# A stored order of tasks, a gate by the tangent, and reciprocals spread by one float32 product

## The chip, the cores and the metric

The kernel runs on one core of one Trainium2 chip. The metric is the device time of one execution, in microseconds; the comparison is between medians of several executions. The core has a matrix engine (TensorE, in the profile PE, with its weight loads as PEld), a vector engine (VectorE, DVE), a scalar engine for activations (ScalarE, ACT), a general engine (GpSimd, POOL) and a queue that issues DMAs (SyncE, SP). Each engine works through its own list of instructions in order and waits on semaphores for the others.

## The reference, cut to what matters

Attention with a positional bias, then a gated block with a short causal convolution (batch 8, 8 heads, sequence 576, head width 64, model width 512):

```python
scores = q @ k.T / 8 + bias            # bias: a two-layer net of log1p distances, 8 heads x 576 x 576
attn = exp(scores - scores.max(-1)); attn /= attn.sum(-1) + 1e-9
x = concat_heads(attn @ v)             # 8 x 576 x 512
gate_pre = sum(conv_w[k] * shift(x, 4 - k) for k in range(5))
gate = 1 / (1 + exp(-gate_pre))
out = (gate * (x @ w_val)) @ w_out
```

## The kernel before, in words

The work falls into tasks. The kernel's text creates them one by one with `add(engines, fn, deps, pri, takes, uses)`: the engines that may run the task, each with a cost, the function that issues its instructions, the tasks it depends on, a priority, and the buffers it takes and uses. Nothing is issued while tasks are created. At the end `Plan.order()` puts all 4162 of them in an order and gives each an engine, and they are issued in that order, so each engine's list is its share of it.

- **Bias**, 36 pieces of 16 rows: `relu` (L374, L376), `bias_mm` (L395), `bias_fin` (L414, L416), `bias_store`.
- **Attention**, 32 `pair(n)`s of two heads of one batch, in 16 runs (`RUNS`, `TRANS`) of two pairs. Per block of 128 query rows: `qkm`/`qkr` (L746, L762) multiply in float32; `logits` (L792, DVE) adds the bias and takes the maximum; `expo` (L804, ACT) exponentiates and sums. Then one of two ways, by `TRANS`. In six runs ("T") `norm` (L857) multiplies by 1/sum, `tp` (L905) transposes on PE and `tev` copies out. In ten runs ("D") the exponentials are split into two float16 parts: `top` (L251 on ACT, L253 on DVE, L255 on POOL) rounds, `rest` and `rest8` (L274, on DVE or POOL) subtract, `swap` transposes by DMA.
- `piece` and `rem_mm` (L974, L1042) multiply with v and `ev` scales the result out. In the D runs 1/sum comes late: `eps` and `recip` (L827, L830) make it, `rh` (L258, L269) and `rl` (L838) split it into two float16 parts, `rb` (L1019; in `rem_mm` L1052) spreads it over partitions by products with a float16 identity, `mu` and `mur` (L1029, L1068) multiply.
- **The gated block** per batch, `mlp`: the convolution (`conv`, `prod`, `acc` at L1114 to L1129, `taps` at L1155 to L1164), `sig` (L1176: the sigmoid, four tiles of 128x576 in one task, in the last batch in four tasks), `split_hi` and `split_lo` (L269, L262, L258, L274), `val` (L1226), `gf` (L1236: the product times a scale per channel `gsc` times the gate), `ghi` and `glo` (L251, L274), `outp` (L1288), `ote` (L1300), `ost`.

`Plan.order()` of the kernel before is a list scheduler: it keeps a clock per engine, counts latencies and costs of its own, and picks by priority. The priorities are tuned numbers (`PAIR_AT`, `PV_AT`, `MLP_AT`, `OFFS`, `LOOK`, `LOAD`). Buffers come from rings (`BUFS`), and the slot a task gets depends on the order too.

```python
def sig(e, ks):
    for k in ks:
        A.activation(out=gates[k].t, in_=gates[k].t, func=AF.Sigmoid)
```

Of the kernel before, what the change touches and what calls it, by code (L numbers as in the profile page):

```python
# [35 lines left out]
SEM, SAME, AHEAD = 0.08, dict(P=0.0, V=0.1, A=0.1, G=0.06, S=0.13), 3.0  # L36
LAT = dict(P=0.16, V=0.08, A=0.09, G=0.03, S=0.0)
SPAN = 3.4
# [3 lines left out]
MLP_AT = (-26, 29, 41, 46, -62, 81, 91, -12)  # L42
PAIR_AT = (-0.25, -8.5, -7.75, -5.5, -7.5, -9, 3.5, -18.5, -6, -0.25, 5.25, 3, -0.5, -3.75, -3.25, -13.25, 7.5, -15, -5.5, -3.25, -8.25, -7.25, 10, 5.5, 13.75, 3, 20.75, 35.75, 32.5, 35.75, 36.25, 48.5)
PV_AT = (-2, -96.5, -90, -28.5, -2.25, -74, -59.75, -8.5, -34.75, -98.25, -19.75, -85, -148.25, -155.25, -53.75, -54.75, 35, -5, -12.75, 64.75, 16.5, -28.75, 24.75, -111, 8.5, 39.75, -12.25, 32.75, 67.5, 21.25, 29.75, -51.25)
TRANS = tuple(x == "T" for x in "TTTTDDDTDDDTDDDD")
# [12 lines left out]
OFFS = dict(qkr=-1.25, ldx=3, swap=-51, qk_ld=-57.75, qkm=5, norm=4, piece=-193, val=-38.5, outp=-128.75, mur=-112.25, bias_store=15.75, conv=-14.25, taps=-12.25, split_hi=-48, rb=30.75, rest=-12, ldv=15.25, w_hi=-57.25, logits=-45.25, relu=-69.5, ost=-236.75, bias_fin=9, ote=-28.5, double_step=-102.25, store=1, ghi=-73.5, sig=-45.5, vtr=-135, recip=-41.25, glo=-8, ev=-66.75, tev=4, evr=-312.75, w_sub=23.75, gf=-165.5, w_ld=-31, mu=-23, w_lo=38.75, bias_mm=-134.5, bias_ld=37.25, expo=-17.25, prod=1.25, vlo=26.25, cw=34, vhi=-0.75, eps=-99.25, vmax=-80.5, acc=1.25, split_lo=11.5, close_bias=-84.5, rem_mm=12.25, top=0, vinv=-26.5, tp=-3.25, vscale=-34, constant=47.25, constant_ev=-204.5, ldm_t=17.25, w_scale=-23.75, bias_ld_t=24.5, qk_ld_t=-52.25, w_max=5.5, cwb=-28, eps_t=-69.5, w_even=-202, ldv_t=23.25, vout=-122.5, vb_store=-79.75, wg_scales=-52, piece_t=-50.75, tp_t=-137, vb_all=62, wg_load=48.25, vmax_t=-102.25, evr_t=62.25, oscale=-56.75, rem_mm_t=45.25, expo_t=-28, vb_max=-170, wg_store=62, w_inv=31.75, recip_t=-178, wg_max=-34.5, qkm_t=4.25, vb_load=-116.25, vmax2_t=-58, norm_t=-8, qkr_t=1.5, ldm=-6, vb_scale=46, wg_inv=58.75, vb_inv=59.75, vmax2=-35.25, logits_t=17.75, ev_t=6.25, tev_t=-169, rl=2, rh=-58.25, rest8=-8.25, wg_mm=32.5, wg_row=52.25, vb_mm=-91)
HOLD = 0.05
STICK = 0  # L60
# [3 lines left out]
RDIV = 2.0**11  # L64
# [11 lines left out]
class Task:  # L76
    def __init__(self, engines, fn, deps, pri, takes):
        self.engines, self.fn, self.deps, self.pri, self.takes = engines, fn, deps, pri, takes
        self.start = self.end = None
        self.late = 0.0  # L80
        self.then = []


class Plan:

# [3 lines left out]
    def add(self, engines, fn, deps=(), pri=0.0, takes=(), uses=(), hold=0.5):  # L94
        name = getattr(fn, "func", fn).__name__
        pri += OFFS.get(name + self.kind, OFFS.get(name, 0.0))
        t = Task(engines, fn, [d for d in deps if d is not None], pri, list(takes))
        t.pri = max([pri] + [d.pri for d in t.deps])
        t.n, t.hold = len(self.tasks), hold
        t.name = name + self.kind  # L100
        t.shares = "GV" if name in SHARED else "G"
        t.mode = MODES.get(name, 0)
        for b in uses:
            b.users.append(t)
        self.tasks.append(t)
        return t

    def order(self):
        free = dict(P=0.0, V=0.0, A=0.0, G=0.0, S=0.0)
        bus = port = 0.0  # L110
        mode, last = 0, None

        pending = {k: [] for k in self.bufs}
        slots = {k: [(0.0, i) for i in range(n)] for k, n in self.bufs.items()}
        for t in sorted(self.tasks, key=lambda t: (t.pri, t.n)):
            t.unmet, t.uses = len(t.deps), []
            t.need = {}
            for b in t.takes:
                pending[b.ring].append(t)
                t.need[b.ring] = t.need.get(b.ring, 0) + 1  # L120
        for t in self.tasks:
            for d in t.deps:
                d.then.append(t)
            for b in t.takes:
                b.left, b.free = len(b.users), 0.0
                for u in b.users:
                    u.uses.append(b)
        def known(t):
            t.known = [
                (e, c, max([0.0] + [d.end + (SAME[e] if d.on == e else SEM + LAT[d.on]) for d in t.deps]))  # L130
                for e, c in t.engines
            ]

        ready = [t for t in self.tasks if not t.unmet]
        for t in ready:
            known(t)
        out = []
        spans, slow, seen = {}, True, 0
        while ready:
            pick = {}  # L140
            for t in ready:
                s = 0.0
                for k, n in t.need.items():
                    spare = len(slots[k]) - n
                    if spare < 0 or t.pri > pending[k][0].pri + LOOK.get(k, 1.0) * spare:
                        s = None
                        break
                    s = max(s, slots[k][n - 1][0])
                if s is None:
                    continue  # L150
                ok, best = s, None
                for e, cost, s in t.known:
                    f = free[e]
                    if e == "S":
                        f = max(f, bus - AHEAD)
                    elif e in t.shares:
                        f = max(f, port - (OVER.get(e, 0.0) if e != last else 0.0))
                    if s < ok:
                        s = ok
                    v = (s if s > f else f) + LOAD[e] * cost  # L160
                    if best is None or v < best[0]:
                        best = v, e, s, f, cost
                _, e, s, f, cost = best
                key = (max(s - HOLD, f), t.pri + STICK * (e == "P" and t.mode != mode), t.n)
                if e not in pick or key < pick[e][0]:
                    pick[e] = (key, max(s, f), t, cost)
            assert pick, "no task can start"
            e = min(pick, key=lambda e: pick[e][1])
            _, s, t, cost = pick[e]
            t.start, t.on = s, e  # L170
            if e == "S":
                bus = max(bus, s + 0.65 + t.hold) + cost
                free[e] = s + t.hold if t.hold < 0.7 else bus - 0.95
                t.end = bus + 0.75 + t.late
            else:
                if e == "P":
                    x = int(s // SPAN)
                    for y in range(seen, x):
                        slow = spans.get(y, 0.0) < WARM[slow] * SPAN
                    seen = x  # L180
                    cost = cost * (2 if slow else 1) + 0.012 + DRAIN * (t.mode != mode)
                    mode = t.mode
                    spans[x] = spans.get(x, 0.0) + min(cost, (x + 1) * SPAN - s)
                    spans[x + 1] = spans.get(x + 1, 0.0) + max(0.0, s + cost - (x + 1) * SPAN)
                free[e] = t.end = s + cost
                if e in t.shares:
                    port, last = t.end, e
            for k in t.need:
                pending[k] = [u for u in pending[k] if u is not t]
            for b in t.takes:  # L190
                _, b.slot = slots[b.ring].pop(0)
# [19 lines left out]
def attention_gated_mlp(  # L211
# [1122 lines left out]
    for t in todo:  # L1334
        t.fn(t.on)
# [53 lines left out]
```

## Time and profile before

| | |
|---|---|
| three executions | 741.88, 743.75 (median), 748.66 us |
| the profiled execution | 747.9 us, its span 746.1 us |
| granted TensorE clock | 0.980 of full speed |
| busy | PE 685.5, DVE 638.5, ACT 615.4, POOL 458.1 us |
| DMA | 125.75 MB in 263303 packets |

A row of a group of instructions gives the line, engine, operation, output and inputs by the program's names, shapes and count; behind the bar the busy time in us and the mean of one in ns; behind the next bar the engine's idle time just before them and what ended it. A row of a source line gives least, median and greatest duration in ns. A row of the timeline or of the chain begins with its start and its length in us. A wait's row has the sum in us, how often, and the longest.

### The profile page before, as it was taken

To read this page: it belongs to the slowest core of one execution; us is meant where nothing else is said; L and a number is where in the kernel's file an instruction comes from. 1 tells how busy PE (TensorE), PEld (TensorE's weight loads), DVE (VectorE), ACT (ScalarE), POOL (GpSimd) and SP (SyncE) were. 2 spreads that over 40 slices of the span, in tenths; PEclk is the share of its full clock that TensorE was granted. 3 is DMA by queue.
4 is the path that set the end of the run, shared out by engine and by line. 5 is a ranking of instruction groups with operands and counts; after the bars stand their busy time and mean duration, and the time that the engine had idled before them with its cause. 6 is when DMAs were issued, how large, how long until landed. Compare 5 with 4: busy or idle time off the path is not lost. (4 is left out here: it accounts for less than half of the span.)

```text
span 746.1 us, 17419 instructions
## 1 busy us (share of the span) xinstructions
PE 685.5 (92%) x6144; PEld 424.3 (57%) x6144; DVE 638.5 (86%) x1709; ACT 615.4 (82%) x1384; POOL 458.1 (61%) x586
## 2 busy tenths in 40 slices
PE   7998989998899999899989898998999989999987
PEld 2334655665665665556655475656666555556653
DVE  7999879999899889988979878998888999879841
ACT  6999777788897978798897988879897987897842
POOL 0002452646688768786468677866687667877752
PEclk9999999999999989999999999999999989999999
DMA  8899912221269689997389899993699998999711
GB/s 263 256 317 298 367 48 93 75 93 50 54 119 209 151 184 194 186 211 136 99 161 219 165 190 196 201 204 99 131 178 215 201 188 171 212 190 174 142 43 58
DMA packets 263303, 125.75 MB, mean 169 GB/s; under 512 B 239792, under 2 KB 240048, under 8 KB 263216
## 3 DMA queue, kind: packets, MB, share of 16 engines
q1 hardware_dynamic: 263072, 124.34, 73.1%
q8 instruction: 49, 0.80, 0.4%
q14 instruction: 38, 0.31, 0.1%
q10 hardware_dynamic: 144, 0.29, 0.1%
HBM read 44.64 MB, written 20.33 MB: 87 GB/s over the span
## 5 line engine op out<-in xcount | busy, mean ns | idle before, releaser
L804 ACT ACTIVATE t_d<-t_d,nm 128x576 f32<-128x576 f32 x288 | 222.8, 775 | 67.3 <-DVE nm L792 63.2
L274 POOL TENSOR_TENSOR t_d<-t_d 128x512 f16<-128x512 f32 (+1 forms) x227 | 219.0, 981 | 77.0 <-ACT t_d L251 71.2
L746 PE MATMUL t_sp<-t_qk 64*128 64x288 f32 x1024 | 192.5, 437 | 22.4 <-DVE nm L792 20.3
L792 DVE CUSTOM_DVE_ANT_0 t_d<-t_sp,bias 128x576 f32<-128x576 f32 x256 | 188.4, 746 | 14.1 <-PE t_sp L746 4.1
L857 POOL TENSOR_SCALAR t_d<-t_d,rinv 128x576 f32<-128x576 f32 x90 | 71.1, 801 | 144.7 <-DVE rinv L830 101.7
L746 PEld LDWEIGHTS t_sp<-t_qk 64*128 64x128 f32 x1024 | 106.3, 187 | 84.1 <-DVE nm L792 43.9
L974 PE MATMUL t_ps<-t_pt,t_w 128*64 128x256 f16 (+1 forms) x1600 | 132.0, 311 | 6.5 <-DMA t_w<-t_w 2.0
L251 ACT CAST t_d<-t_d 128x576 f16<-128x576 f32 x162 | 105.9, 662 | 2.8 <-DVE t_d L274 1.5
L1226 PEld LDWEIGHTS <-wv 128*128 128x128 f16 x768 | 72.6, 99 | 33.3 <-issue 13.4
L905 PE MATMUL t_ps<-ident,t_d 128*128 128x128 f32 x486 | 70.2, 285 | 11.7 <-ACT t_pt L251 5.3
L1226 PE MATMUL t_ps<-xh,wv 128*128 128x320 f16 (+1 forms) x512 | 77.6, 291 | 0.5 <-ACT t_xp L251 0.5
L905 PEld LDWEIGHTS t_ps<-ident,t_d 128*128 128x128 f32 x486 | 53.7, 143 | 35.7 <-issue 11.2
L974 PEld LDWEIGHTS <-t_w 128*64 128x64 f16 x1120 | 59.2, 112 | 17.6 <-issue 14.2
L1164 DVE SCALAR_TENSOR_TENSOR t_ps<-t_xp,convw,t_ps 128x288 f32<-128x288 f32 x126 | 65.2, 517 | 2.1 <-ACT t_ps L1155 0.2
L1288 PE MATMUL t_ps<-wo,gh 128*128 128x512 f16 x256 | 62.8, 385 | 3.1 <-ACT gh L251 3.1
L251 ACT COPY t_pt<-t_ps 128x512 f32<-128x512 f32 (+1 forms) x120 | 56.3, 512 | 4.2 <-PE t_ps L905 3.9
L804 ACT ACTIVATION_READ_ACCUMULATOR t_d<-t_d,nm 128x1 f32 x288 | 55.4, 192 | 0.0
L395 PE MATMUL t_ps<-rel,w 128*32 128x288 f32 (+17 forms) x352 | 49.2, 490 | 1.7 <-DVE rel L376 1.1
L274 POOL TENSOR_TENSOR gl<-t_w,gh 128x256 f16<-128x256 f32 x52 | 38.0, 731 | 20.0 <-ACT gh L251 19.5
L376 DVE TENSOR_SCALAR rel<-gt,sct,nb 128x576 f32<-128x576 f32 (+17 forms) x108 | 46.3, 507 | 0.0
L974 PEld LDWEIGHTS t_ps<-t_pt,t_w 128*64 128x64 f32 x480 | 31.7, 136 | 25.8 <-issue 6.3
L1236 DVE SCALAR_TENSOR_TENSOR t_w<-t_ps,gsc,t_w 128x256 f32<-128x256 f32 (+1 forms) x64 | 32.5, 510 | 14.3 <-PE t_ps L1226 13.7
(141 smaller groups left out, 1077.4 us busy)
## 6 DMA issues: line engine op xcount, KB each, us to landing
t_qk<-qkd SPq DMA_DIRECT2D x32, 576.0 KB, 4.2
bias_d<-t_be SPq DMA_DIRECT2D x36, 295.5 KB, 4.9
bias<-bias_d SPq DMA_DIRECT2D x16, 576.0 KB, 6.8
out<-t_w SPq DMA_DIRECT2D x32, 256.0 KB, 2.4
t_w<-vd SPq DMA_DIRECT2D x20, 320.0 KB, 4.0
t_w<-vn SPq DMA_DIRECT2D x12, 320.0 KB, 5.1
t_d<-wvd SPq DMA_DIRECT2D x4, 512.0 KB, 6.1
t_d<-wod SPq DMA_DIRECT2D x4, 512.0 KB, 3.6
```

Source lines behind the costliest of these rows:

```text
L251: A.copy(out=out, in_=in_)
L274: (V if e == "V" else G).tensor_tensor(out=out, in0=in0, in1=in1, op=ALU.subtract)
L395: T.matmul(pb[32 * g : 32 * g + 32, 0 : y - x], lhsT=w28, rhs=rel[g].t[:, x:y], start=True, stop=True, tile_position=(0, 32 * g),)
L746: T.matmul(ts[a][:, j, 0:hw], lhsT=qk.t[r, c * P : (c + 1) * P], rhs=qk.t[r, x : x + hw], start=True, stop=True,)
L792: V.tensor_tensor_reduce(out=part(c, a).rearrange("p (j f) -> p j f", j=2), in0=sp.t[:, :, 0 : S // 2], in1=bias.rearrange("p (j f) -> p j ...
L804: A.activation(out=part(c, a), in_=part(c, a), func=AF.Exp, bias=nms[c][:, a : a + 1], scale=-1.0, accum_out=sums[c][:, a, 0:1],)
L857: (G if e == "G" else V).tensor_scalar(out=t, in0=t, scalar1=rinvs[c][:, a : a + 1], scalar2=1.0, op0=ALU.mult, op1=ALU.mult,)
L905: T.transpose(t[:, k * P : (k + 1) * P], es[c].t[:, (k0 + k) * P : (k0 + k + 1) * P], ident)
L974: T.matmul(po.t[r, 0:256], lhsT=vt.t[:, v, r], rhs=pt[:, x, :, :] if tr else pt[:, :, x, :], start=(t == 0 and m == 0), stop=(t == 4 and m ...
L1164: V.scalar_tensor_tensor(out=o, in0=x, scalar=wt, in1=t, op0=ALU.mult, op1=ALU.add)
L1226: T.matmul(pm.t[:, 0:w], lhsT=weights["wv"][wi][:, k, d * P : (d + 1) * P], rhs=xb.t[xi][:, k, 0:w], start=(q == 0 and k == 0), stop=(q == ...
L1288: T.matmul(pm.t, lhsT=gb.t[gi][:, k, o : o + P] if o < 256 else gx.t[gi][:, k, :], rhs=weights["wo"][wi][:, k, :], start=(q == 0 and k == ...
```

## The change

The sigmoid becomes (1 + tanh(x/2)) / 2: the activation is the hyperbolic tangent with scale 0.5, and a new task `half` computes `gsc * t + gsc` with `gsc` halved, so that `gf` multiplies two tensors only. It is created for each of a batch's four gate tiles, on POOL, ACT or DVE, and `sig` is now four tasks in every batch. In the D runs `rh` and `rl` go, and `rb` and the last part of `rem_mm` multiply the float32 reciprocals with the float32 identity. `eps` may run on POOL too. `Plan.order()` reads the order and the engines from a stored string of 4115 entries, two bytes per task; priorities and costs no longer act. The kind of run is "TTTTDDDDTDDDTDDD" in place of "TTTTDDDTDDDTDDDD": the two later T runs each come one run later.

```diff
+ORDER = (
...
-                    for x in range(2):
-                        for a, r in enumerate(halfs):
-                            T.matmul(
-                                t[r, D:P],
-                                lhsT=rhl[NM][x][:, a : a + 1].to_broadcast([P, D]),
-                                rhs=ident16[:, o],
...
+                    for a, r in enumerate(halfs):
+                        T.matmul(
+                            t[r, D:P],
+                            lhsT=rinvs[NM][:, a : a + 1].to_broadcast([P, D]),
+                            rhs=ident[:, o],
...
-                A.activation(out=gates[k].t, in_=gates[k].t, func=AF.Sigmoid)
...
+                A.activation(out=gates[k].t, in_=gates[k].t, func=AF.Tanh, scale=0.5)
+
+        def half(e, k):
+            g, c = gates[k].t, gsc[:, k : k + 1]
+            if e == "A":
+                A.activation(out=g, in_=g, func=AF.Identity, scale=c, bias=c)
+            else:
+                (V if e == "V" else G).tensor_scalar(out=g, in0=g, scalar1=c, scalar2=c, op0=ALU.mult, op1=ALU.add)
+
+        sg = []
+        for k in range(NK):
+            x = st + (4 + 3 * k if final else 14) * per
+            y = add([("A", 0.61)], partial(sig, ks=[k]), [convs[k]], x)
+            sg.append(add([("G", 0.77), ("A", 0.78), ("V", 0.5)], partial(half, k=k), [y] + wdone, x + 0.3))
...
+        code = zlib.decompress(base64.b85decode("".join(ORDER)))
+        n = len(code) // 2
+        assert n == len(self.tasks)
+        for lo, hi in zip(code[:n], code[n:]):
+            t = self.tasks[(lo + 256 * hi) // 4]
+            assert not t.done and all(d.done for d in t.deps)
+            t.on, t.done = t.engines[lo % 4], True
```

Unpacked and set against the tasks by name, the stored string puts the tasks that may run on several engines as follows (the counts before are those of the trace):

| task | before, ACT / DVE / POOL | stored, ACT / DVE / POOL |
|---|---|---|
| `top` | 162 / 1 / 17 | 139 / 10 / 31 |
| `rest` | - / 28 / 152 | - / 48 / 132 |
| `norm` | - / 18 / 90 | - / 14 / 94 |
| `eps` | - / 104 / - | - / 59 / 45 |
| `acc` | - / 9 / 27 | - / 19 / 17 |
| `split_hi` | 47 / 2 / 15 | 41 / 8 / 15 |
| `ghi` | 45 / 5 / 14 | 30 / 11 / 23 |
| `glo` | - / 12 / 52 | - / 22 / 42 |
| `sig` | 32 tiles / - / - | 32 / - / - |
| `half` | | 28 / - / 4 |

More of the change, by code (lines that the diff above doesn't have):

```diff
@@ L41 @@
 WEIGHTS = (8, 4)
[L42 to L45, printed above, removed]
+MLP_AT = (8, 51, 32, 37, -19, 62, 70, -128)
@@ L76, with __init__ @@
 class Task:
[L77 to L81, printed above, removed]
+    def __init__(self, engines, fn, deps, takes):
+        self.engines, self.fn, self.deps, self.takes = [e for e, _ in engines], fn, deps, list(takes)
+        self.uses, self.done = [], False
 class Plan:
@@ L94, in add @@
     def add(self, engines, fn, deps=(), pri=0.0, takes=(), uses=(), hold=0.5):
[L95 to L102, printed above, removed]
+        t = Task(engines, fn, [d for d in deps if d is not None], takes)
         for b in uses:
@@ L108, in order @@
     def order(self):
[L109 to L117, printed above, removed]
-            for b in t.takes:
-                pending[b.ring].append(t)
-                t.need[b.ring] = t.need.get(b.ring, 0) + 1
@@ L121, in order @@
[L121 to L125, printed above, removed]
+        slots = {k: list(range(n)) for k, n in self.bufs.items()}
+        for t in self.tasks:
+            for b in t.takes:
+                b.left = len(b.users)
                 for u in b.users:
                     u.uses.append(b)
[L128 to L189, printed above, removed]
-            for b in t.takes:
-                _, b.slot = slots[b.ring].pop(0)
-            for u in t.then:
-                u.unmet -= 1
-                if not u.unmet:
-                    known(u)
-                    ready.append(u)
@@ L197, in order @@
+        code = zlib.decompress(base64.b85decode("".join(ORDER)))
[5 more added lines that the diff above has]
+            t.on, t.done = t.engines[lo % 4], True
+            for b in t.takes:
+                b.slot = slots[b.ring].pop(0)
             for b in t.uses:
                 b.left -= 1
-                b.free = max(b.free, t.end + SEM + LAT[t.on])
@@ L200, in order @@
                 if not b.left:
-                    slots[b.ring].append((b.free, b.slot))
-                    slots[b.ring].sort()
-            ready.remove(t)
-            out.append(t)
-        assert len(out) == len(self.tasks)
-        self.length = max(t.end for t in out)
-        return out
+                    slots[b.ring].append(b.slot)
+            yield t
 @with_exitstack
@@ L340, in constant_ev @@
             V.tensor_copy(out=cadd[32 * g : 32 * g + 32, :], in_=pc.t[32 * g : 32 * g + 32, 0:1])
-    ident16 = cp.tile([P, P], F16, name="ident16")
-    G.tensor_scalar(out=ident16, in0=ident, scalar1=1.0 / RDIV, scalar2=1.0, op0=ALU.mult, op1=ALU.mult)
     consts = add([("P", 0.1)], constant, (), -20, [pc])
@@ L721, in pair @@
         halves = [Buf("pt"), Buf("pt")]
-        nms, rinvs, rhl, sm, invs, rsum = {}, {}, {}, None, {}, {}
+        nms, rinvs, sm, invs, rsum = {}, {}, None, {}, {}
         es, inv = {}, {}
@@ L821, in eps @@
                             invs["t"] = smp.tile([P, 10], F32, name="rinvs", tag="rinvs", bufs=10)
-                            invs["h"] = [smp.tile([P, 10], F16, name="rhl", tag=f"rhl{y}", bufs=10) for y in range(2)]
                             for y in range(NM + 1):
-                                rhl[y] = [z[:, 2 * y : 2 * y + 2] for z in invs["h"]]
+                                rinvs[y] = invs["t"][:, 2 * y : 2 * y + 2]
                         o, u = invs["t"][:, x : x + w], sm[:, x : x + w, :]
                     inv[c] = o
-                    V.tensor_reduce(out=o, in_=u, op=ALU.add, axis=AX.X)
+                    if e == "V":
+                        V.tensor_reduce(out=o, in_=u, op=ALU.add, axis=AX.X)
+                    else:
+                        G.tensor_tensor(out=o, in0=u[:, :, 0], in1=u[:, :, 1], op=ALU.add)
                 def recip(e, c=c):
                     V.reciprocal(out=inv[c], in_=inv[c])
-                def rh(e, x):
-                    z = invs["t"][:, x]
-                    scaled_copy(e, invs["h"][0][:, x], z, RDIV)
-                def rl(e, x):
-                    z = invs["t"][:, x]
-                    V.scalar_tensor_tensor(
-                        out=invs["h"][1][:, x], in0=z, scalar=RDIV, in1=invs["h"][0][:, x], op0=ALU.mult, op1=ALU.subtract
-                    )
                 key = (hg, l, c) if c < NM else (hg, 0, c)
@@ L1015, in rb @@
             def rb(e, g=g, po=po):
-                for c, x in ((c, x) for c in range(2) for x in range(2)):
+                for c in range(2):
                     for a, r in enumerate(halfs):
@@ L1020, in rb @@
                             po.t[r, 256 + c * P : 256 + (c + 1) * P],
-                            lhsT=rhl[2 * g + c][x][:, a : a + 1].to_broadcast([P, D]),
-                            rhs=ident16,
-                            start=x == 0,
-                            stop=x == 1,
+                            lhsT=rinvs[2 * g + c][:, a : a + 1].to_broadcast([P, D]),
+                            rhs=ident,
+                            start=True,
+                            stop=True,
                         )
@@ L1029, in mu @@
                 V.tensor_tensor(out=o, in0=o, in1=po.t[:, 256:512], op=ALU.mult)
[L1031 removed]
+            x = add([("P", 0.48)], rb, [last, rsum[g]], d + 1.2, (), [po])
             x1 = add([("V", 0.34)], mu, [x0, x], d + 2, (), [po])
@@ L1212, in mlp @@
                 )
-                u = add([("V", 0.47), ("G", 1.25)], split_lo, [h], base + 0.3 * k + 0.2, (), [xp])
+                u = add([("V", 0.53 if pi == 0 else 0.6), ("G", 1.2 if pi == 0 else 1.4)], split_lo, [h], base + 0.3 * k + 0.2, (), [xp])
                 hs.append(h)
@@ L1332, in attention_gated_mlp @@
             done += 1
-    todo = plan.order()
-    for t in todo:
+    for t in plan.order():
         t.fn(t.on)
```

154 lines of the change are left out of this document (95 added, 59 removed).

## The prediction

> **What bounds the kernel now.** I read the page's busy line and chain first, then the busy times by stage, then the waits.
>
> ```profile
> span 746.1 us, 17419 instructions
> PE 685.5 (92%) x6144; PEld 424.3 (57%) x6144; DVE 638.5 (86%) x1709; ACT 615.4 (82%) x1384; POOL 458.1 (61%) x586
> ...
> DVE 13%; ACT 11%; PE 10%; issue 4%; DMA 3%; POOL 1%; DVEq 0%; ACTq 0%; POOLq 0%
> ```
>
> No engine is full. The chain that ended last (it is followed back to 419.65 us, so its shares add up to about 42% of the span) passes DVE, ACT and PE almost equally, with no single place that holds it.
>
> ```profile
> 65.00:190.00 125.00, 113.79 (x924) 73.92 (x925) 114.24 (x347) 99.60 (x240) 61.18 (x73) 0.99 0.39 127
> ...
> 550.00:690.00 140.00, 131.26 (x1251) 82.12 (x1250) 124.66 (x321) 120.85 (x265) 106.27 (x129) 0.96 0.97 195
> 690.00:746.10 56.10, 46.38 (x404) 28.59 (x401) 27.51 (x51) 28.92 (x64) 27.50 (x32) 0.95 0.35 81
> ```
>
> The columns are stretch, length, busy PE, PEld, DVE, ACT, POOL, granted clock, DMA share, GB/s. Up to 690 us DVE is busy 638.5 - 27.5 = 611.0 of 690 us, 88.5%; in the stage 65 to 190 it reaches 114.24 / 125 = 91.4%. The last 56 us are the last batch's gated block, where PE leads and DVE and ACT are half idle. In 550 to 690 the DMA engines are also nearly full (0.97).
>
> ```profile
> POOL t_d L274 <- ACT t_d L251: 71.2, 56, 4.4
> ACT t_d L804 <- DVE nm L792: 63.2, 68, 3.6
> ...
> PE t_sp L746 <- DVE nm L792: 20.3, 28, 1.5
> ```
>
> These are one ring: DVE makes logits, ACT exponentiates and splits them, POOL subtracts, PE waits for DVE to free the logits banks. PE is the fullest, but what it waits for is DVE. So I price the elementwise work, and treat PE as a limit that must not be passed.
>
> **The change part by part.** *Gate.* Sigmoid becomes tanh(x/2), a further pass `half`, and a plain product in `gf`.
>
> ```profile
> 655.79 0.66 ACT L251 CAST t_d<-t_d 128x576 f16<-128x576 f32 x1
> 656.47 1.28 ACT L1176 ACT_TABLE_LOAD   x1
> 657.76 2.40 ACT L1176 ACTIVATE t_w<-t_w 128x576 f32<-128x576 f32 x4
> ```
>
> ```profile
> L1176 ACT ACT_TABLE_LOAD x8 | 10.3, 1283 | 0.1
> L804 ACT ACT_TABLE_LOAD x7 | 9.0, 1283 | 0.1
> ...
> L1118 ACT ACTIVATE t_w<-t_xp,convw 128x576 f32<-128x576 f32 x9 | 6.9, 768 | 1.8 <-DVE t_xp L1068 1.6
> ```
>
> Each batch loads a table ahead of the sigmoids (L1176) and, seven times, another ahead of the next exponential (L804). The load starts when the cast ends (656.45) and the sigmoid when the load ends (657.75): its whole price is 1.28 us. If tanh and exp share a table, 10.3 + 9.0 = 19.3 us leave ACT. The 32 tanh passes cost what 32 sigmoids did. Added are 32 passes over 128x576; the stored table puts 28 on ACT and 4 on POOL. An ACT pass of that size with one per-partition operand takes 0.768 us (L1118): 28 x 0.768 = 21.5 us on ACT, 3 us on POOL (0.75 each, the nearest ACT price). `gf` does one multiplication fewer; I count nothing for it.
>
> ```profile
> L1236 DVE SCALAR_TENSOR_TENSOR t_w<-t_ps,gsc,t_w 128x256 f32<-128x256 f32 (+1 forms) x64 | 32.5, 510 | 14.3 <-PE t_ps L1226 13.7 <-ACT t_w L1176 0.4
> ```
>
> The wait that `half` adds is `gf`'s on DVE, with logits queued behind it and ACT and PE behind those. Today `gf` waits 0.4 us for the sigmoid: the gate is early, and one pass more costs nothing there while it stays a few microseconds early. In the last batch nothing covers it: up to four passes, 3 us, of which I count none apart from ACT's load. No DMA is added; the transposes go out behind `rest` as before.
>
> The Trainium skill, "ScalarE: Activation LUTs", section "Table sets: the hidden batching unit", lists tanh in the set of exp, and its section "What ACT_TABLE_LOAD costs" prices a switch at about 2.66 us with a drain. By the page 15 switches would be an estimated 40 us; the trace shows no drain beside the 1.28 us, and I stay with the trace.
>
> *Reciprocals.* The split of 1/sum into two float16 parts goes.
>
> ```profile
> L838 DVE SCALAR_TENSOR_TENSOR rhl<-rinvs,rhl x50: 145/392/1157, 213.0 to 698.9; 128x4 f16<-128x4 f32 x40, 128x2 f16<-128x2 f32 x10
> ...
> L258 DVE TENSOR_SCALAR rhl<-rinvs x22: 165/379/1161, 238.2 to 695.3; 128x4 f16<-128x4 f32 x18, 128x2 f16<-128x2 f32 x4
> ```
>
> ```profile
> L838 DVE SCALAR_TENSOR_TENSOR rhl<-rinvs,rhl 128x4 f16<-128x4 f32 (+1 forms) x50 | 24.6, 493 | 1.4 <-ACT rhl L269 0.9 <-POOL rhl L258 0.2
> ...
> L258 DVE TENSOR_SCALAR rhl<-rinvs 128x4 f16<-128x4 f32 (+1 forms) x22 | 11.1, 507 | 0.6
> ...
> L269 ACT ACTIVATE rhl<-rinvs 128x4 f16<-128x4 f32 (+1 forms) x26 | 5.2, 202 | 3.9 <-DVE rinvs L830 3.9
> ```
>
> DVE loses 24.6 + 11.1 = 35.7 us, ACT 5.2 us. But these instructions hold two to four columns: at their shortest they take 0.145 and 0.165 us, 50 x 0.145 + 22 x 0.165 = 10.9 us. The other 24.8 us is time in which a tiny operation stood still. Whether that vanishes or falls on the next DVE operation bounds the saving to 10.9 to 35.7 us. I take 35.7: what follows on DVE is mostly a logits pass that reads PSUM. The Trainium skill, "SBUF — State Buffer", section "SBUF: two separate sides", says that DVE operations with two SBUF inputs or in a two-port mode and POOL operations lock each other out for whole instructions. The minima and maxima agree; by that rule the wait would pass on to a `rest` or an `acc` that follows, and that is the slower rival below.
>
> On PE four float32 products replace eight float16 ones per `rb`; a float32 product is two passes, so again eight.
>
> ```profile
> L1019 PE MATMUL t_ps<-ident,rhl 128*64 128x128 f16 x320 | 15.6, 220 | 0.1
> ...
> L974 PE MATMUL t_ps<-t_pt,t_w 128*64 128x256 f16 x1120 | 71.6, 279 | 3.5 <-DMA t_w<-t_w 2.0 <-DVE t_xp L1029 0.8 <-DMA t_pt<-t_d 0.7
> ...
> L974 PE MATMUL t_ps<-t_pt,t_w 128*64 128x256 f32 x480 | 60.4, 387 | 2.9 <-DVE t_xp L253 2.0 <-ACT t_pt L251 0.7
> ...
> L620 PE MATMUL t_ps<-ident,bsc 128*128 128x128 f32 x16 | 3.7, 313 | 1.7 <-DVE bsc L617 1.7
> ```
>
> With 64-wide weights and 256 columns one float32 pass takes 60.4 / 480 = 0.126 us; for 128 columns half, 0.063, so 320 passes are 20 us against 15.6: +4.6. By the lonely pairs of L620 (3.7 / 16 = 0.231 us) they would be 74 us: +58. The kind of tile is that of L974, so I take +8 with the remainder's products. A gain is excluded: as many passes, each on wider data.
>
> *Places and engines.* The stored table has one entry per task. Counted by task name, it moves work among engines too:
>
> ```profile
> L251 ACT CAST t_d<-t_d 128x576 f16<-128x576 f32 x162 | 105.9, 662 | 2.8 <-DVE t_d L274 1.5 <-POOL t_d L274 0.6
> ...
> L255 POOL TENSOR_SCALAR t_d<-t_d 128x576 f16<-128x576 f32 x17 | 11.8, 696 | 7.5 <-ACT t_d L804 3.3 <-ACT gh L251 1.6 <-POOL t_d L274 1.4
> ...
> L253 DVE CAST t_d<-t_d 128x576 f16<-128x576 f32 x1 | 0.5, 546 | 0.0
> ```
>
> ```profile
> L274 POOL TENSOR_TENSOR t_d<-t_d 128x512 f16<-128x512 f32 x152 | 183.3, 1214 | 76.6 <-ACT t_d L251 71.0 <-issue 1.2 <-POOL gxl L274 0.8
> ...
> L274 DVE TENSOR_TENSOR t_d<-t_d 128x512 f16<-128x512 f32 x28 | 25.6, 914 | 7.7 <-ACT t_d L251 7.3
> ```
>
> ```profile
> L1129 POOL TENSOR_TENSOR t_w<-t_w 128x576 f32<-128x576 f32 x27 | 38.6, 1430 | 4.0 <-ACT t_w L1124 2.7
> ...
> L1129 DVE TENSOR_TENSOR t_w<-t_w 128x576 f32<-128x576 f32 x9 | 9.2, 1023 | 2.9 <-POOL t_w L1129 2.1 <-POOL t_w L1126 0.6
> ...
> L827 DVE TENSOR_REDUCE rinv<-sm 128x2 f32<-128x4 f32 x54 | 8.1, 150 | 9.2 <-ACT t_d L804 8.9
> ...
> L827 DVE TENSOR_REDUCE rinvs<-sm 128x4 f32<-128x8 f32 (+1 forms) x50 | 7.7, 153 | 13.9 <-ACT t_d L804 13.5
> ...
> L685 POOL TENSOR_SCALAR vsc<-vcol 128x1 f32<-128x1 f32 x10 | 2.5, 250 | 3.0 <-DVE vcol L681 2.0 <-DVE rinvs L827 0.4
> ```
>
> `top` goes from 162/1/17 on ACT/DVE/POOL to 139/10/31, `rest` from 28/152 on DVE/POOL to 48/132, `acc` from 9/27 to 19/17, and 45 of 104 `eps` go to POOL. Sums:
> - ACT: -19.3 - 5.2 - 23 x 0.662 + 21.5 = -18.2 us
> - DVE: -35.7 - 45 x 0.152 + 20 x 0.914 + 10 x 1.023 + 9 x 0.546 = -9.1 us
> - POOL: -20 x 1.214 - 10 x 1.430 + 14 x 0.696 + 45 x 0.250 + 3 = -14.6 us
>
> Moves of under ten tasks, or between like prices, are left to the range.
>
> **Two sums.** *By load:* -42 us of 638.5 + 615.4 + 458.1 = 1712 is 2.5%; at the same packing 746.1 x 0.025 = 18 us. *By chain:*
>
> ```profile
> 422.48 0.87 DVE rhl L838
> ...
> 511.40 1.28 ACT L1176
> ...
> 696.42 0.55 DVE rhl L838
> ...
> 698.81 1.28 ACT L1176
> ```
>
> Between 419.65 and the end the chain holds five table loads, 6.4 us, and twelve pieces of the split (first and last shown), 6.6 us: 13 us in 326. The gate and split run from about 188 us, 558 us in all: 13 x 558 / 326 = 22 us if nothing else was as late. Against it stand `half`, 21.5 us at ACT's part of the chain (11 of 42): 5.6 us, and PE's 8 at 10 of 42: 2 us. That leaves -14.5 us. Behind a load that goes, the next late thing is the logits pass that ACT waits for (63.2 us), so I don't take the 22 whole. Between 14.5 and 18 I take 16.5. The profiled execution took 747.9 us (1.8 us around its span), 4 above the median of the three runs, 743.75; taken off that median, as the comparison is of medians: **727 us**, 2.2% faster.
>
> **Rivals.** A kernel of this kind can be told from no change at about 1%, 7.4 us.
> 1. *The stored order also packs better.* If DVE were as full up to the tail as it is in 65 to 190: (611.0 - 9.1) / 0.914 + 56.1 = 715 us of span, 31 less: **712**. For it: POOL's and ACT's long waits are of ordering. Against: DMA at 0.97 in 550 to 690 moves the same bytes in any order.
> 2. *The freed time turns into other waits.* PE is 92% busy and gains 8 us; 693.5 at 92 to 93% is a span of 746 to 754: no change, **744 to 750**. For it: the chain's equal shares. Against: PE's own waits are for DVE.
> 3. *Slower: DVE becomes the bound.* Place: DVE's queue ahead of the logits, where it now takes `rest` and `acc` from POOL. If all 24.8 us of standing still pass on, DVE has 638.5 - 9.1 + 24.8 = 654; at today's 86%, 764 us of span: **762**. It turns the sign where more than 9.1 us pass on. Against: POOL itself has less to lock with.
> 4. *Slower: PE becomes the bound* by L620's price: 685.5 + 58 = 743 busy, at 95% a span of 783: **780**.
> 5. *The tables still switch.* The table of places sets tanh passes singly among the exponentials; were the sets different, each of 32 would need two loads, 49 more than today, 63 us: ACT 680 busy, at 86% a span of 790: about **788**.
>
> **How the numbers follow.** Forecast (717 to 736) 0.43; rival 1 0.25, 0.06 of it under 704; rival 2 0.19; rivals 3, 4, 5 0.08, 0.03, 0.02. Faster by over 1% is 0.68, within 1% 0.19, slower 0.13. The range 704 to 750 leaves 0.06 below and 0.14 above.
>
> **What would show it.** After: one table load at the start; no `rhl` rows; 28 `half` passes near 0.77 us on ACT; `rest` on DVE still near 0.9 us; the float32 `rb` passes under 0.1 us each; DVE near 629, ACT near 597, POOL near 444 us busy; ACT's wait for `nm` not above 63 us. Wrong it would be if DVE's `rest` or the logits passes grew (the wait passed on), if PE's waits for `nm` grew past 20.3 us, or if the order left the engines clearly fuller or emptier than today's 86% on DVE.

## The result and the profile after

The changed kernel takes **723.06 us** (median of four runs, 720.91 to 725.42) against 745.01 us (741.88 to 748.66) for the kernel before: a ratio of 0.9704, 95% interval 0.9648 to 0.9761. The profiled execution took 725.42 us, against 747.9 before. The four runs were granted a TensorE clock of 0.987 to 0.995 of full speed; the kernel before got 0.980 in its profiled execution. One execution of the kernel before, beside the experiments, took 812.61 us at a clock of 0.752; no number below rests on it.

The page's head, busy line and chain of the changed kernel:

```profile
span 723.6 us, 17323 instructions
...
PE 673.0 (93%) x6144; PEld 421.0 (58%) x6144; DVE 639.4 (88%) x1656; ACT 593.6 (82%) x1323; POOL 446.5 (62%) x624
...
PE 19%; DMA 3%; DVE 3%; ACT 2%; POOL 2%; issue 1%; SPq 0%; ACTq 0%; POOLq 0%; DVEq 0%
```

DVE is as busy as before (639.4 against 638.5 us), in a span 22.5 us shorter; ACT has lost 21.8 us, POOL 11.6, PE 12.5. The chain, which was shared by DVE, ACT and PE, is now mostly PE; it reaches back over some 30% of the span, where the one before reached over some 42%.

Busy time by stage (stretch, length, PE, PEld, DVE, ACT, POOL, clock, DMA share, GB/s):

```profile
65.00:190.00 125.00, 119.13 (x973) 79.88 (x973) 116.83 (x328) 102.71 (x258) 76.27 (x106) 0.97 0.43 143
...
550.00:670.00 120.00, 112.75 (x1095) 71.83 (x1091) 108.23 (x263) 107.01 (x231) 88.02 (x118) 1.00 0.93 183
670.00:723.60 53.60, 48.78 (x402) 30.09 (x398) 36.18 (x79) 27.36 (x56) 19.88 (x29) 0.99 0.45 103
```

Up to the tail DVE is busy (639.4 - 36.2) / 670 = 90.0% of the time, where it was 88.5%. The last stretch is cut by hand, at 670 us here and at 690 before, and it holds more of DVE's work now (36.2 us against 27.5), so the lengths of the two are not compared.

The waits (engine, tile and line, what it waited for; us, times, longest):

```profile
POOL t_d L231 <- ACT t_d L208: 55.1, 48, 4.3
...
ACT t_d L758 <- DVE nm L746: 39.4, 48, 4.4
...
DVE t_d L746 <- PE t_sp L700: 15.6, 26, 2.4
...
PE t_sp L700 <- DVE nm L746: 7.4, 8, 3.4
```

The row of the kernel before that answers to the third:

```profile
DVE t_d L792 <- PE t_sp L746: 4.1, 9, 0.7
```

ACT's wait for `nm` fell from 63.2 to 39.4 us and PE's from 20.3 to 7.4; DVE's wait for PE's logits (`t_sp`) rose from 4.1 to 15.6. Between PE and DVE the waiting has turned round: DVE now waits longer for PE's logits than PE for DVE. ACT still waits for DVE most.

### The profile page after: what moved, and what is told of

It reads as the page before. It is cut to its first block, busy times and chain, and to the rows that moved or that the text cites. A ratio compares the mean times of both kernels' runs of the same rounds, so it can differ in the third digit from the quotient of the medians.

```text
span 723.6 us, 17323 instructions
## 1 busy us (share of the span) xinstructions
PE 673.0 (93%) x6144; PEld 421.0 (58%) x6144; DVE 639.4 (88%) x1656; ACT 593.6 (82%) x1323; POOL 446.5 (62%) x624
## 5 line engine op out<-in xcount | busy, mean ns | idle before, releaser
L758 ACT ACTIVATE t_d<-t_d,nm 128x576 f32<-128x576 f32 x288 | 222.2, 774 | 45.1 <-DVE nm L746 39.4
L231 POOL TENSOR_TENSOR t_d<-t_d 128x512 f16<-128x512 f32 (+1 forms) x203 | 193.2, 969 | 71.6 <-ACT t_d L208 55.1
L746 DVE CUSTOM_DVE_ANT_0 t_d<-t_sp,bias 128x576 f32<-128x576 f32 x256 | 186.2, 749 | 25.2 <-PE t_sp L700 15.6
L700 PE MATMUL t_sp<-t_qk 64*128 64x288 f32 x1024 | 179.8, 433 | 9.9 <-DVE nm L746 7.4
L700 PEld LDWEIGHTS t_sp<-t_qk 64*128 64x128 f32 x1024 | 101.6, 187 | 60.9 <-DVE nm L746 24.9
L803 POOL TENSOR_SCALAR t_d<-t_d,rinv 128x576 f32<-128x576 f32 x94 | 74.3, 801 | 43.6 <-DVE rinv L786 17.7
L208 ACT CAST t_d<-t_d 128x576 f16<-128x576 f32 x139 | 91.0, 667 | 8.0 <-DVE t_d L231 2.5
L208 ACT COPY t_pt<-t_ps 128x512 f32<-128x512 f32 (+1 forms) x123 | 53.8, 480 | 11.3 <-PE t_ps L848 11.0
L349 PE MATMUL t_ps<-rel,w 128*32 128x288 f32 (+17 forms) x352 | 46.1, 487 | 6.6 <-DVE rel L330 3.0
L231 DVE TENSOR_TENSOR t_d<-t_d 128x512 f16<-128x512 f32 (+1 forms) x67 | 48.5, 737 | 2.9 <-POOL t_d L212 1.5
L231 POOL TENSOR_TENSOR gl<-t_w,gh 128x256 f16<-128x256 f32 x42 | 29.3, 699 | 25.9 <-ACT gh L208 20.4
```

Source lines behind the costliest of these rows:

```text
L208: A.copy(out=out, in_=in_)
L231: (V if e == "V" else G).tensor_tensor(out=out, in0=in0, in1=in1, op=ALU.subtract)
L700: T.matmul(ts[a][:, j, 0:hw], lhsT=qk.t[r, c * P : (c + 1) * P], rhs=qk.t[r, x : x + hw], start=True, stop=True,)
L746: V.tensor_tensor_reduce(out=part(c, a).rearrange("p (j f) -> p j f", j=2), in0=sp.t[:, :, 0 : S // 2], in1=bias.rearrange("p (j f) -> p j ...
L758: A.activation(out=part(c, a), in_=part(c, a), func=AF.Exp, bias=nms[c][:, a : a + 1], scale=-1.0, accum_out=sums[c][:, a, 0:1],)
L803: (G if e == "G" else V).tensor_scalar(out=t, in0=t, scalar1=rinvs[c][:, a : a + 1], scalar2=1.0, op0=ALU.mult, op1=ALU.mult,)
```

## The experiments

Two families. Names with f_ start from the kernel before with its tasks, order and engines as they were; names with s_ start from the changed kernel with its stored order; r_fold alone plans anew. Every one computes the whole reference. Ratios are to the kernel before, run beside them on the same chip. The experiments were run in three sets, and the result in another; the kernel before had a median between 745.0 and 746.4 us in all of them, so a difference between medians of two sets carries 1 to 2 us of doubt from this alone. In the expectations, theory 1 says that the work that left is the gain; theory 2 says that the stored order is, and that in the old order the freed time turns into waits. Where a measured time lies outside what was expected, the text says so.

| kernel | order | reciprocals | gate | median us | ratio (95%) |
|---|---|---|---|---|---|
| f_recip | old | float32 | sigmoid | 726.77 | 0.9725 (0.9669 to 0.9781) |
| f_gate | old | split | tanh, second pass | 751.96 | 1.0071 (1.0033 to 1.0110) |
| f_both | old | float32 | tanh, second pass | 737.92 | 0.9884 (0.9822 to 0.9947) |
| f_fold, f_fold2 | old | float32 | tanh, folded | 721.48, 720.91 | 0.9667 (0.9625 to 0.9709), 0.9653 (0.9611 to 0.9694) |
| f_unread | old | float32, split still run | sigmoid | 746.28 | 0.9991 (0.9963 to 1.0019) |
| r_fold | planned anew | float32 | tanh, folded | 755.93 | 1.0104 (1.0068 to 1.0140) |
| after2 (changed kernel again) | stored | float32 | tanh, second pass | 724.14 | 0.9675 (0.9638 to 0.9713) |
| s_oldgate | stored | float32 | sigmoid | 770.28 | 1.0308 (1.0252 to 1.0363) |
| s_split | stored | split | tanh, second pass | 736.57 | 0.9868 (0.9821 to 0.9915) |
| s_oldeng | stored places, old engines | float32 | tanh, second pass | 785.87 | 1.0532 (1.0490 to 1.0574) |
| s_fold | stored | float32 | tanh, folded | 727.59 | 0.9753 (0.9706 to 0.9799) |

### The parts one at a time in the old order

**f_recip**: the reciprocals alone. The two split tasks keep their places in the plan but issue nothing; `rb` and its remainder read the float32 reciprocals.

```diff
-                    scaled_copy(e, invs["h"][0][:, x], z, RDIV)
+                    return
...
-                for c, x in ((c, x) for c in range(2) for x in range(2)):
+                for c in range(2):
...
-                            rhs=ident16,
+                            rhs=ident,
```

> The old order frozen, with the float32 reciprocals alone. DVE is rid of 72 instructions that took 35.7 us. If their standing still goes with them, DVE is busy about 603 us and the kernel 9 to 12 us faster (theory 1); if it passes on to the next instruction that meets POOL, DVE stays above 620 us and the gain is under 4 us (the slower rival of the prediction). PE: 400 float32 passes, 20 to 31 us in place of 20. Theory 2: under 3 us either way.

Measured 726.77 us, ratio 0.9725: **19.6 us**, nearly all that the whole change brings, and more than either of the two gains expected. DVE's busy time is the one expected by theory 1. Its busy line, and then three rows of its groups (busy, mean ns, idle time ahead and what ended it):

```profile
PE 679.3 (93%) x6144; PEld 425.0 (58%) x6144; DVE 606.6 (83%) x1637; ACT 610.8 (84%) x1358; POOL 459.5 (63%) x584
```

```profile
L792 DVE CUSTOM_DVE_ANT_0 t_d<-t_sp,bias 128x576 f32<-128x576 f32 x256 | 187.7, 747 | 20.2 <-DMA t_pt<-t_d 11.7 <-PE t_sp L746 5.8 <-PE t_ps L902 0.7
...
L274 DVE TENSOR_TENSOR t_d<-t_d 128x512 f16<-128x512 f32 x28 | 24.5, 876 | 9.4 <-ACT t_d L251 9.0
...
L274 DVE TENSOR_TENSOR t_d<-t_d 128x128 f16<-128x128 f32 x15 | 7.5, 498 | 0.0
```

DVE lost 638.5 - 606.6 = 31.9 of the split's 35.7 us. Nearly none of the standing still passed on: `rest` on DVE takes 876 ns (914 before) and a logits pass 747 (746 before). What did come back, 3.8 us in all, is in small rows such as `rest8`, 498 ns where it took 409.

**f_gate**: tanh, a second pass on ACT right behind the four of a batch, and the plain product in `gf`. In the first batch, where the scale comes late, the pass stands just ahead of `gf`.

```diff
-                A.activation(out=gates[k].t, in_=gates[k].t, func=AF.Sigmoid)
+                A.activation(out=gates[k].t, in_=gates[k].t, func=AF.Tanh, scale=0.5)
+            if late:
+                return
+            for k in ks:
+                half(k)
+
+        def half(k):
+            c = gsc[:, k : k + 1]
+            A.activation(out=gates[k].t, in_=gates[k].t, func=AF.Identity, scale=c, bias=c)
```

> The old order frozen, with the gate by tanh alone (second pass on ACT behind the four tanh passes; in the first batch just ahead of the product). 15 table loads of 1.28 us leave ACT, 32 passes of about 0.7 us come: ACT's work hardly changes. Theory 1: at chain prices -11 us for the loads and +6 for the passes, so 3 to 6 us faster. Theory 2: no difference, within 3 us.

Measured 751.96 us, 0.7% **slower**, where either a gain or no difference was expected. Its groups and one of its waits:

```profile
L1184 ACT ACTIVATE t_w<-t_w,gsc 128x576 f32<-128x576 f32 x32 | 25.7, 857 | 0.1
```

```profile
DVE t_w L1246 <- ACT t_w L1184: 4.5, 4, 1.3
```

The 15 loads (19.3 us) are gone, but 32 passes at 857 ns put 25.7 us in their place, in one piece behind each batch's tanh. `gf`, which waited 0.4 us for ACT, now waits 4.5. Its products themselves became cheaper, 28.8 us on DVE where they took 32.5, which the prediction counted as nothing.

**f_both**: the two edits together, in the old order. It does the changed kernel's work; what differs is where and on which engines tasks run, which runs are T, and that the second pass always stands on ACT, in one piece with the tanh ahead of it.

```diff
-                    scaled_copy(e, invs["h"][0][:, x], z, RDIV)
+                    return
...
-                A.activation(out=gates[k].t, in_=gates[k].t, func=AF.Sigmoid)
+                A.activation(out=gates[k].t, in_=gates[k].t, func=AF.Tanh, scale=0.5)
...
+            A.activation(out=gates[k].t, in_=gates[k].t, func=AF.Identity, scale=c, bias=c)
```

> The order and the engines of the kernel before, frozen (the same tasks are planned, and the two that split the reciprocals issue nothing), with both edits of the arithmetic: tanh with its second pass on ACT, and float32 reciprocals. Theory 1, the work that left is the gain: it is 14 to 18 us faster than before, about 728 us, and the stored order brings the remaining 4 to 8 us. Theory 2, the stored order is the gain, and in the old order the freed time turns into waits: within 7 us of before, 738 to 748 us.

Measured 737.92 us, 11.2 above f_recip, at the edge of theory 2's range; but neither theory holds, since the reciprocals gain and the gate loses. So from before to after, one step at a time: reciprocals -19.6, gate +11.2, and what is left to the stored order, 723.06 - 737.92 = **-14.9 us** (13.4 by the two ratios). This last step holds the places, the engines, the two moved T runs and the places of the second pass together.

### Why the reciprocals pay

**f_unread** runs the split as before, but nothing reads it: `rb` takes the float32 reciprocals, as early as in f_recip. It tells engine time from an earlier reciprocal.

```diff
-                                rhl[y] = [z[:, 2 * y : 2 * y + 2] for z in invs["h"]]
+                                rhl[y] = invs["t"][:, 2 * y : 2 * y + 2]
```

> The old order with the float32 reciprocals, but the split is still computed on the engines that had it, and nothing reads it. PE's products wait for the reciprocal only, as in the run with the float32 reciprocals alone (726.8). If that run gained because DVE no longer stands still in the split: the gain is gone, 741 to 749 us, DVE busy about 638. If it gained because the reciprocal reaches PE two instructions sooner: 725 to 731, whatever DVE's busy time.

```profile
L838 DVE SCALAR_TENSOR_TENSOR rhl<-rinvs,rhl 128x4 f16<-128x4 f32 x40 | 22.0, 550 | 0.7 <-ACT rhl L269 0.3 <-POOL rhl L258 0.2
```

Measured 746.28 us against 746.35 for the kernel before beside it: nothing, as expected if the gain is engine time. The earlier reciprocal and the dearer products together are worth nothing. f_unread and f_recip differ in nothing but the split's own instructions, so these are what the 19.5 us between the two pay for: in the kernel before, 35.7 us on DVE, 5.2 on ACT and two instructions on POOL.

One thing goes along with it that no run parts from it. f_recip was granted a TensorE clock of 0.988 to 0.994 of full speed, f_unread 0.975 to 0.983. Over 36 executions of the kernel before, between 740.7 and 751.8 us, the time falls by about 5.6 us for each 0.01 of granted clock. By that slope, which makes it an estimate, some 6 of the 19.5 us go with the clock. Whether the time fell because the clock was higher, or the clock was higher because DVE kept PE waiting less, is not shown.

**s_split** puts the split back into the changed kernel, on DVE right behind the reciprocal, with the eight float16 products.

```diff
+                        scaled_copy("V", h[0][:, x], z, RDIV)
+                        V.scalar_tensor_tensor(
+                            out=h[1][:, x], in0=z, scalar=RDIV, in1=h[0][:, x], op0=ALU.mult, op1=ALU.subtract
+                        )
```

> The stored order with the float16 split of the reciprocals put back: two more DVE instructions in each of the 50 late reciprocals, eight float16 products per rb. In the old order the split's removal alone made 20 us. Theory 1, the split's standing still is time of DVE wherever it lies: 30 to 40 us of DVE again, 672 us in all, and 12 to 22 us slower than the changed kernel, 735 to 745. Theory 2, the stored order has slack at the late reciprocals: under 6 us slower.

```profile
PE 679.9 (92%) x6144; PEld 420.0 (57%) x6144; DVE 672.0 (91%) x1756; ACT 593.8 (80%) x1323; POOL 446.6 (61%) x625
```

Measured 736.57 us, ratio 0.9868: 13.5 us above the changed kernel, as theory 1 expected, for 32.6 us more on DVE; ACT and POOL are as busy as in the changed kernel. That is 0.4 us of time for each us of DVE in this order, and 19.5 / 31.9 = 0.6 in the old one.

### The gate, the order and the engines

**s_oldgate**: the stored order with sigmoid, no second pass, and `gf` as before.

```diff
-                A.activation(out=gates[k].t, in_=gates[k].t, func=AF.Tanh, scale=0.5)
+                A.activation(out=gates[k].t, in_=gates[k].t, func=AF.Sigmoid)
...
-            g, c = gates[k].t, gsc[:, k : k + 1]
...
+            return
```

> The stored order with the old gate: sigmoid, no second pass, the scale back in the product. Since the stored order sets the 32 gate passes singly among the exponentials, tables are loaded for nearly each: 40 to 64 loads, 51 to 82 us of ACT, against 22 us of passes saved. Theory 1 and 2 alike: slower than the changed kernel by 15 to 45 us, about 740 to 765 us. If it is as fast as the changed kernel, the tangent was of no use to it.

```profile
L1118 ACT ACT_TABLE_LOAD x28 | 35.9, 1283 | 0.5
...
L758 ACT ACT_TABLE_LOAD x27 | 34.6, 1283 | 0.5
```

Measured 770.28 us, **47 us slower** than the changed kernel, a little more than the 15 to 45 that were expected. The stored order sets gate passes singly among exponentials: 55 switches, 70.5 us, against 23.8 us of second passes that ACT is spared. This order pays only with a gate that needs no other table than exp; with tanh the changed kernel loads one table in all.

**s_oldeng**: the stored places, but 401 tasks on the engine that they had before.

```diff
-            t.on, t.done = t.engines[lo % 4], True
+            t.on, t.done = t.engines[OTHER.get((lo + 256 * hi) // 4, lo % 4)], True
```

> The changed kernel in its stored order, but each task on the engine that it had in the kernel before, where both have it (401 tasks change engine; the runs whose kind differs and the second gate pass keep theirs). It tells places from engines. If the balance of engines is what the table brings, the 15 us between the old order with both edits (738) and the changed kernel (723) come back: 733 to 742. If the places are, it stays under 730.

```profile
PE 691.1 (88%) x6144; PEld 424.3 (54%) x6144; DVE 619.3 (79%) x1643; ACT 615.5 (79%) x1363; POOL 453.5 (58%) x589
```

Measured 785.87 us, far beyond both of the expected ranges. DVE is 20 us less busy than in the changed kernel, ACT 22 us and PE 18 us more, and the time is 63 us longer. In this order the engines belong to the places; which of the 401 moves costs the time was not parted.

**s_fold** and **f_fold** drop the second pass: `gf` computes (tanh + 1) times its product in one DVE instruction, and the channel's factor is multiplied into the rows of w_out once; powers of two move between the scales of x and the weights (not shown). s_fold does it in the stored order, f_fold in the old order with float32 reciprocals.

```diff
+        w = weights["wo"][x][:, k, :]
+        scalars(e, w, w, gsc[:, k : k + 1], 1.0)
...
-                        in0=pm.t[:, 0:w],
-                        scalar=gsc[:, d : d + 1],
-                        in1=gates[d].t[:, t0 : t0 + w],
-                        op0=ALU.mult,
+                        in0=gates[d].t[:, t0 : t0 + w],
+                        scalar=1.0,
+                        in1=pm.t[:, 0:w],
+                        op0=ALU.add,
```

> The changed kernel without the second gate pass: the product on DVE adds 1 to the tangent while it multiplies, the factor per channel goes into the rows of w_out once, and the powers of two into the scales of x and w_val. ACT loses 28 passes, 23.8 us, POOL 3.4; DVE's products cost 3 to 4 us more. If ACT's load sets the pace as much as DVE's: 6 to 10 us faster than the changed kernel, 713 to 717. If the stored order has those passes in ACT's slack: within 3 us, 720 to 726.

> The old order frozen, float32 reciprocals, tangent, and no second gate pass, as in s_fold. Against the float32 reciprocals alone (726.8) ACT loses 15 table loads, 19 us, and nothing comes. If the second pass is what made the tangent a loss in the old order: 716 to 722. If it is the tangent in those places: 727 or more.

Busy lines, s_fold and then f_fold:

```profile
PE 675.0 (93%) x6144; PEld 422.0 (58%) x6144; DVE 641.9 (88%) x1662; ACT 573.7 (79%) x1295; POOL 445.7 (61%) x622
```

```profile
PE 677.9 (94%) x6144; PEld 424.2 (59%) x6144; DVE 605.6 (84%) x1642; ACT 591.1 (82%) x1343; POOL 462.0 (64%) x587
```

s_fold: 727.59 us, **not faster** than the changed kernel although ACT has 19.9 us less; both expected ranges lie lower. f_fold: 721.48 us, as expected, 16.4 below f_both. The pass costs 16 us as it stands in the old order and nothing in the stored one. The two differ in more than the order: in f_both the four passes of a batch stand in one piece on ACT, in the stored order each has a place of its own and four of the 32 are on POOL. The old order with the passes placed singly was not run. Why s_fold came out some 4 us higher was not settled; the intervals overlap, and it has 2.5 us and six instructions more on DVE, those that scale the rows of w_out.

**after2** and **f_fold2** repeat the two best beside each other; nothing is edited: after2 is the changed kernel and f_fold2 is f_fold.

> The changed kernel again, on the chip of the runs beside it: 720 to 726 us.

> The old order with both edits and no second gate pass again, to hold it against the changed kernel on one chip: if the stored order is worth nothing by itself, the two are within 4 us, 718 to 726.

```profile
PE 678.3 (95%) x6144; PEld 425.0 (59%) x6144; DVE 605.4 (84%) x1642; ACT 591.0 (82%) x1343; POOL 461.6 (64%) x587
...
PE 47%; DVE 20%; ACT 14%; DMA 11%; issue 4%; POOL 2%; SPq 1%; POOLq 0%; DVEq 0%; ACTq 0%
```

724.14 and 720.91 us, as expected; the intervals, 0.9638 to 0.9713 and 0.9611 to 0.9694, overlap. No version beats the changed kernel measurably; f_fold2 ties with it by another road, with 34 us less on DVE and PE 95% busy.

**r_fold** is f_fold with the two empty split tasks taken out of the list, so that the planner decides anew with the old priorities.

```diff
-                        x = add([("A", 0.22), ("G", 0.22), ("V", 0.12)], partial(rh, x=z), [x], h + 2.3)
-                        rsum[g] = add([("V", 0.13)], partial(rl, x=z), [x], h + 2.4)
+                        rsum[g] = x
```

> As f_fold, but planned anew by the old scheduler without the two tasks of the split, so that places and engines fit the work that is left. If a plan that fits its work is worth what the misfit of the second pass cost: 712 to 718. If the old priorities were tuned to the old set of tasks and a new plan is a throw of the dice: 718 to 735.

```profile
PE 697.9 (92%) x6144; PEld 435.0 (58%) x6144; DVE 618.1 (82%) x1666; ACT 594.8 (79%) x1339; POOL 451.6 (60%) x570
```

Measured 755.93 us, 35 us above f_fold2 with the same arithmetic, and 21 above the most that was expected. The old priorities gave a poor plan for this list of tasks: with less to do it was slower than the kernel before. It is one plan; how others by the same priorities would fare is not known.

## Why the prediction was right, and where its terms were off

The time, 727, was 4 us high: the kernel is 3.0% faster where 2.2% was expected. Errors of opposite sign hide in that, and that they nearly cancel is luck. In the prediction's chain sum the reciprocals gave 11 less 2 for PE, 9 us; the gate 11 less 5.6, 5.4 us; the order nothing. Measured one step at a time, the reciprocals gave 19.6, the gate cost 11.2 and the order gave 14.9 (23.3 in sum, against 22.0 between the medians of the result). Gate and order together gave 3.7 where 5.4 was expected, but the prediction had the sign of the gate wrong in the old order and no term for the order.

- **The split, taken at 35.7 us on DVE: right as engine time.** DVE lost 31.9 in f_recip, and neither `rest` nor the logits passes grew; rival 3 (762) falls. How it works is to be seen in the kernel before, in one stretch of its timeline (start, length), DVE and then POOL:

```profile
610.79 1.08 DVE L838 SCALAR_TENSOR_TENSOR rhl<-rinvs,rhl 128x4 f16<-128x4 f32 x1
611.79 0.74 DVE L792 CUSTOM_DVE_ANT_0 t_d<-t_sp,bias 128x576 f32<-128x576 f32 x1
```

```profile
610.70 1.15 POOL L274 TENSOR_TENSOR t_d<-t_d 128x512 f16<-128x512 f32 x1
```

The four-column instruction ends with POOL's (611.87 and 611.85), and the logits pass stands behind it: 1.08 us for work that takes 0.145 at the least. It is the rule: of the split's 72 instructions on DVE 44 took over 0.3 us, and 28 of these end within 0.04 us of the end of one POOL instruction; at the end of each of the other 16 the timeline shows two POOL instructions as one row. In the Trainium skill, "SBUF — State Buffer", section "SBUF: two separate sides", the lock is held for the whole instruction and the other side blocks; this row agrees. That the wait would then fall on the next DVE operation, which the prediction read from it, did not happen in f_recip, but for the 3.8 us above.

- **The split's share of the time, by chain: mis-sized.** Twelve pieces, 6.6 us, scaled by 558 / 326 gave 11 us; it was worth 19.5 (13.5 in the stored order). Read in short windows, the chain holds 21 pieces of the split with ACT's, 7.5 us, which scale to 13: still too little. A likely reason is that a delay on DVE also sets when ACT and PE get their next work, which the one chain that ends last counts only where it happens to pass; the granted clock is another. No run parts them.
- **The table loads: mis-sized the other way.** 6.4 us scaled to 11; taking them out without a second pass moved f_recip's 726.77 to f_fold's 721.48, 5.3 us, with intervals that overlap. Not all of it need be the loads: the same edit takes 4.1 us off `gf` on DVE and puts 2.9 on it for w_out.
- **The second pass: mis-sized.** Priced at 0.768 us from L1118, which has one per-partition operand; this one has two. Groups of the changed kernel:

```profile
L1123 ACT ACTIVATE t_w<-t_w,gsc 128x576 f32<-128x576 f32 x28 | 23.8, 859 | 0.1
...
L1118 ACT ACTIVATE t_w<-t_w 128x576 f32<-128x576 f32 x32 | 21.6, 677 | 3.7 <-DVE t_w L1106 3.6
...
L962 PE MATMUL t_ps<-ident,rinvs 128*64 128x128 f32 x320 | 25.3, 281 | 7.1 <-ACT t_xp L226 7.1
...
L231 DVE TENSOR_TENSOR t_d<-t_d 128x512 f16<-128x512 f32 x48 | 38.7, 809 | 2.9 <-POOL t_d L212 1.5 <-ACT t_d L208 1.1
...
L231 DVE TENSOR_TENSOR gl<-t_w,gh 128x256 f16<-128x256 f32 x22 | 13.5, 615 | 0.2
...
L210 DVE CAST gh<-t_w 128x256 f16<-128x256 f32 x11 | 7.0, 632 | 0.2
...
L1071 DVE TENSOR_TENSOR t_w<-t_w 128x576 f32<-128x576 f32 x19 | 14.2, 751 | 0.2
...
L279 ACT ACT_TABLE_LOAD x1 | 1.3, 1283 | 1.1 <-PEq L1320 1.1
```

None (the tanh pass), one and two operands give 677, 768 and 859 ns: 91 each. By the Trainium skill, "ScalarE: Activation LUTs", section "What ACT_TABLE_LOAD costs" (186 ns, 0.833 per column, 93 per such operand), two would be an estimated 852; the trace agrees. The 5.6 us that it was to cost in time were too few for the old order (16.4) and too many for the stored one (nothing).
- **One table load in all**, as expected: rival 5 (788) falls. What it feared is real where the sets differ: s_oldgate, 770. The same section's 2.66 us for a switch would be an estimated 146 us of ACT for its 55; the trace does not agree: its rows show 1.283 each, 70.5 us in all, with 1.0 us idle ahead of all 55, and ACT is 52 us busier than in the changed kernel.
- **PE +8: the term was 11.3** (25.3 + 6.3 for the products and the remainder's, against 15.6 + 4.7), 0.079 us a pass where 0.063 was taken. Rival 4 (780) falls. PE's total fell all the same, by 12.5 us, so other rows lost 24; half of it is the logits' row. Before:

```profile
L746 PE MATMUL t_sp<-t_qk 64*128 64x288 f32 x1024 | 192.5, 437 | 22.4 <-DVE nm L792 20.3 <-DVE t_xp L996 1.2 <-issue 0.5
...
L274 DVE TENSOR_TENSOR gl<-t_w,gh 128x256 f16<-128x256 f32 x12 | 6.7, 559 | 1.2 <-ACT gh L251 1.0
...
L253 DVE CAST gh<-t_w 128x256 f16<-128x256 f32 x5 | 1.7, 340 | 0.0
```

After:

```profile
L700 PE MATMUL t_sp<-t_qk 64*128 64x288 f32 x1024 | 179.8, 433 | 9.9 <-DVE nm L746 7.4 <-DMA t_qk<-qkd 2.0 <-DVE t_w L1182 0.4
```

One takes about as long as before (433 against 437 ns), and together they keep PE busy for 12.7 us less, so they overlap more. Why is not shown; the granted clock differs too (0.980 and 0.987).
- **Sums by engine.** ACT 593.6 (597 expected) and POOL 446.5 (444) were near; DVE 639.4 against 629. The step that missed is "Moves of under ten tasks, or between like prices, are left to the range": `gl` went from 6.7 to 13.5 us and `gh` from 1.7 to 7.0, 12 us of moves that the table of tasks under the change already shows, and `glo`, with ten tasks more on DVE, belonged in the sum even by that rule. The miss looks smaller than it is, because two terms were too dear: `rest` added 13.1 us where 18.3 stood and `acc` 5.0 where 10.2 stood (means of 809 and 751 ns, 914 and 1023 before).
- **Rival 1, better packing (712): half of it came.** DVE went from 88.5% to 90.0% ahead of the tail, not to 91.4, and the order is worth 14.9 us on its own work (f_both against after). But the second pass costs 16.4 us in the old order: against f_fold, the best kernel in the old order, which does without the pass, the stored order gains nothing that can be measured.
- **Rival 2, other waits: not so far.** PE is busy for 93% of the span (95% in f_fold2) and DVE waits for it 15.6 us; PE is the place to look at for the next step.

So 727 came near 723 by the right main cause, the split, counted at about half, and by a stored order, counted at nothing, that pays for the pass which the tangent adds.

## What to carry to other kernels

Look for tiny instructions on a full engine whose mean is several times their minimum: their price is the standing still, and taking them out gave 31.9 of 35.7 us back here. A chain names places but doesn't price a removal: for the split it gave about half, for the table loads about twice what was measured. Where order and engines were fitted by hand or by search, they belong to one list of tasks: measure an edit in both orders, since a pass cost 16 us as placed in one and nothing in the other, and a new plan by old priorities cost 35. And read the granted clock beside every time: in these experiments every kernel under 730 us ran at 0.982 of full speed or more, every one over 740 us at 0.984 or less.

## What the runs showed of the hardware that was not expected

A DVE instruction on four columns can last as long as the POOL instruction that it meets: for L838 0.145 us at the least, 0.392 in the median, 1.157 at the most, and 35.7 us for all 72 instructions of the split on DVE. With them gone, neither `rest` nor the logits passes became slower, and 3.8 us came back in smaller rows. An ACT pass over 576 columns grows by 91 ns with each per-partition operand. One float32 pass of 64-wide weights on 128 columns takes 25.3 / 320 = 0.079 us of busy PE, against 15.6 / 320 = 0.049 for a float16 one.
